# Two transformer layers with a sliding window: four attention blocks of the second layer taken in pairs

## The chip, the cores and the metric

The kernel runs on one core of one Trainium2 chip. The metric is the device time of one execution in microseconds, the median of several runs. The core's engines run side by side, each with an instruction queue of its own: TensorE (PE, with PEld for loading its stationary operand), VectorE (DVE), ScalarE (ACT), GpSimd (POOL) and SyncE (SP), which here only issues DMA transfers. An instruction that needs another engine's result waits for a semaphore, and everything behind it in its queue waits with it.

## The reference

Two attention layers and two MLPs alternate, with the same weights in both layers. S is 2048, D is 512, there are 32 heads of 16, and F is 1792.

```python
def _A_ref(x, wqkv, wo):
    B, S, D = x.shape
    H = 32; Dh = D // H; W = 256
    qkv = (lambda x, *d: x.transpose(*d))((x @ wqkv).reshape(B, S, 3, H, Dh), 2, 0, 3, 1, 4)
    q, k, v = qkv[0], qkv[1], qkv[2]
    scores = jnp.einsum("bhqd,bhkd->bhqk", q, k) * (Dh ** -0.5)
    idx = jnp.arange(S)
    mask = (idx[:, None] - idx[None, :] >= 0) & (idx[:, None] - idx[None, :] < W)
    scores = jnp.where(mask[None, None], scores, -1e9)
    p = _softmax(scores, axis=-1)
    o = jnp.einsum("bhqk,bhkd->bhqd", p, v)
    return (lambda x, *d: x.transpose(*d))(o, 0, 2, 1, 3).reshape(B, S, D) @ wo
...
x = x + _A_ref(_layernorm(x, axis=-1), A_wqkv, A_wo)
x = x + _B_ref(_layernorm(x, axis=-1), B_w1, B_b1, B_w2, B_b2)
```

The last two lines run twice. `_B_ref` is `gelu(h @ w1 + b1) @ w2 + b2` with the tanh form of gelu. A query sees itself and the 255 keys before it.

## The kernel before

**Tiles and blocks.** The 2048 tokens are 16 tiles of 128. Both layers together have 32 tiles (numbered 0 to 31) and 16 blocks of 256 queries (0 to 15); blocks 8 to 15 are the second layer. The 32 heads lie in four groups of eight (c = 0 to 3); a group's 128 channels fill the partitions.

**One block of attention (L730).** Keys are cut into tiles of 64. Key tile m of a block, counted from the block's first query, runs from -4 to 3 and meets the queries that `cols_of` (L707) gives it: 64 to 256 of them. The eight key tiles of a head group have 1280 columns together. They are packed into *visits* of exactly 512 columns (`pieces_of`, L711): ten visits per block, which hold 2, 2, 3, 3 and 6 (head group, key tile) units, twice over. In a visit PE does four matmuls of 32 rows per unit (L754), for the four pairs of heads of the group; two banks of PSUM at a time are then turned by ACT into exponentials in the ring E (L761, two instructions per visit), and masks of zeros and ones are multiplied onto the 64-column segments that lie on an edge of the window, by DVE or POOL (L782). When the five visits of two head groups are there, one product with V (L804, 128 small matmuls of 64 rows and 17 columns, the 17th a column of ones that gives the softmax sum) is made for both groups; then DVE transposes it out of PSUM (L813), takes reciprocals (L817), DVE or POOL normalises (L821), and DVE transposes again into OT (L827).

**Around it.** The output projection (`outproj`, L844) takes four matmuls per tile of 128 queries, and DVE adds the result to X (L849). Then follow the statistics on DVE (L599, L601), the reciprocal root on POOL (L611, L617), the normalised copy (L627) and a DMA transpose into xnTB (L632), which the MLP reads. The MLP runs in *jobs* of two or four tiles (`mlp`, L853; `JOBS`, L460); of the second layer's, tiles 16 to 19, 20 to 23 and 24 to 27 are jobs of four, 28 and 29 and 30 and 31 jobs of two. A job multiplies with w1 (L863), takes the gelu on ACT (L874, L879), multiplies with w2 (L892) and adds on DVE (L894); the second layer's tiles are then stored (L898). Tile 31 is done in two halves of 256 columns (L889). Q, K and V of a block are made two blocks ahead (L661, L680). All dense matmuls go through one helper and show as L653.

**Order.** Every instruction, or group of them, is a numbered node. `_ORDER` (L167) is one list of all node numbers, written out; each engine's queue is that list with the other engines' nodes left out. `_ALT` (L331) names the nodes that go to their second engine (masks and normalisations from DVE to POOL, some copies from PSUM to ACT, one step of the layer norm from POOL to DVE). `_BANKS` (L343) gives the PSUM bank of each group. The semaphores that a node waits for follow from what it reads and writes; a node waits for all of them before its first instruction. The product with V is one such node, and so is a visit.

Of the kernel before, what the change touches and what calls it, by code (L numbers as in the profile page):

```python
# [19 lines left out]
class _Sched:  # L20
# [147 lines left out]
    15, 34, 5, 0, 6, 14, 35, 7, 33, 28, 38, 29, 47, 8, 18, 23, 9, 36, 3, 26, 31, 10, 57, 37, 11, 22, 1, 40, 4, 24,  # L168
    2, 58, 59, 61, 17, 42, 62, 21, 60, 65, 41, 63, 19, 64, 68, 55, 32, 66, 107, 39, 69, 67, 20, 105, 50, 70, 3097,
    48, 30, 27, 53, 25, 106, 108, 71, 109, 49, 72, 110, 73, 16, 74, 114, 81, 75, 82, 111, 83, 84, 115, 85, 86, 116,  # L170
    112, 87, 88, 89, 113, 195, 153, 117, 127, 128, 151, 196, 129, 130, 154, 118, 152, 131, 119, 197, 155, 120, 156,
    98, 99, 100, 121, 12, 101, 90, 13, 102, 367, 91, 368, 104, 159, 92, 93, 157, 94, 103, 325, 76, 369, 199, 77,
    326, 95, 78, 200, 79, 370, 132, 80, 133, 96, 134, 135, 201, 323, 97, 203, 198, 137, 136, 158, 138, 205, 144,
    139, 202, 140, 145, 204, 141, 146, 160, 147, 122, 520, 217, 148, 123, 206, 124, 219, 143, 125, 208, 126, 46,
    218, 324, 43, 213, 209, 327, 328, 215, 166, 167, 168, 331, 169, 214, 207, 371, 176, 329, 177, 521, 373, 210,
    178, 330, 216, 179, 522, 171, 172, 180, 372, 161, 173, 211, 142, 174, 170, 56, 375, 220, 162, 376, 332, 163,
    164, 523, 175, 524, 221, 374, 377, 150, 212, 165, 149, 380, 378, 222, 188, 382, 189, 44, 190, 181, 45, 525,
    182, 381, 223, 385, 183, 224, 191, 386, 184, 384, 226, 225, 227, 54, 231, 232, 387, 379, 233, 526, 234, 383,
    333, 228, 185, 343, 388, 389, 334, 192, 229, 235, 344, 395, 194, 230, 335, 396, 345, 238, 346, 291, 390, 236,
    397, 239, 237, 347, 240, 336, 241, 348, 337, 349, 338, 242, 350, 244, 339, 243, 391, 399, 351, 401, 340, 341,  # L180
    352, 400, 245, 403, 342, 392, 402, 51, 353, 405, 52, 354, 355, 398, 356, 186, 360, 404, 357, 361, 362, 527,
    363, 393, 408, 364, 253, 409, 260, 261, 407, 254, 262, 410, 359, 413, 255, 246, 247, 415, 411, 256, 412, 257,
    248, 249, 250, 258, 414, 406, 564, 251, 273, 394, 274, 566, 263, 276, 416, 267, 268, 417, 565, 264, 270, 271,
    265, 277, 642, 285, 286, 423, 567, 418, 640, 275, 643, 528, 287, 529, 428, 272, 419, 282, 252, 283, 429, 288,
    259, 289, 641, 420, 308, 290, 309, 421, 424, 266, 310, 311, 279, 278, 644, 269, 422, 645, 284, 307, 280, 312,
    281, 313, 314, 315, 540, 425, 426, 568, 427, 541, 570, 316, 648, 542, 543, 649, 317, 569, 544, 318, 530, 531,
    319, 532, 187, 533, 572, 534, 193, 320, 574, 321, 646, 430, 431, 322, 647, 292, 573, 293, 294, 432, 577, 295,
    435, 579, 366, 576, 296, 545, 297, 436, 358, 571, 298, 433, 578, 546, 582, 434, 547, 437, 584, 548, 575, 550,
    438, 899, 551, 552, 650, 583, 553, 439, 651, 441, 652, 440, 653, 554, 900, 897, 585, 592, 654, 299, 549, 300,
    301, 593, 365, 302, 303, 304, 442, 581, 305, 594, 586, 535, 536, 898, 580, 596, 537, 306, 598, 538, 587, 901,  # L190
    539, 902, 597, 595, 600, 588, 557, 601, 660, 661, 662, 663, 599, 602, 605, 664, 558, 559, 607, 560, 655, 656,
    561, 457, 458, 606, 603, 610, 903, 657, 589, 658, 612, 904, 604, 453, 590, 459, 454, 476, 455, 477, 611, 485,
    486, 563, 609, 479, 591, 480, 482, 562, 613, 659, 470, 471, 483, 556, 905, 464, 465, 467, 478, 468, 484, 608,
    450, 460, 469, 461, 906, 451, 466, 446, 452, 447, 481, 443, 487, 448, 444, 473, 472, 462, 665, 474, 456, 614,
    666, 667, 445, 463, 615, 449, 475, 616, 684, 625, 626, 668, 617, 489, 686, 620, 618, 490, 491, 492, 685, 493,
    619, 621, 494, 669, 688, 687, 627, 690, 628, 622, 629, 495, 488, 623, 689, 496, 632, 692, 497, 694, 498, 624,
    691, 499, 500, 501, 630, 502, 693, 697, 504, 631, 505, 633, 1017, 506, 698, 507, 508, 634, 509, 1018, 510, 503,
    635, 699, 511, 702, 1019, 670, 512, 704, 700, 671, 672, 1020, 695, 673, 1021, 703, 674, 712, 696, 513, 514,
    701, 676, 714, 515, 706, 516, 517, 705, 518, 713, 519, 716, 638, 707, 717, 715, 718, 833, 720, 708, 721, 677,
    917, 1022, 918, 919, 709, 722, 920, 719, 710, 725, 921, 678, 727, 679, 680, 724, 681, 726, 730, 922, 636, 923,  # L200
    1023, 731, 912, 924, 728, 1024, 913, 723, 914, 915, 732, 729, 925, 711, 941, 637, 943, 734, 907, 908, 909, 733,
    910, 916, 926, 555, 735, 942, 639, 1025, 911, 736, 945, 934, 946, 935, 675, 737, 947, 738, 683, 949, 1026, 936,
# [763 lines left out]
```

## Time and profile before

| | |
|---|---|
| median of 3 runs | 442.32 us (442.26 to 442.40) |
| profiled execution, its own span | 442.4 us (442.375 us from the first to the last instruction) |
| granted clock of TensorE, mean | 0.996 of full speed |
| ACT_TABLE_LOAD instructions on ACT | 19, of 1.28 us each, nearly all at a change between exponential and gelu |
| score visits / products with V | 150 / 32 |
| mask instructions | 125 on DVE, 111 on POOL |

"Busy" is the time in which an engine has an instruction in work. Matmuls overlap: one of 512 columns is shown with about 0.38 us although the next begins 0.22 us after it, so what a group of matmuls costs is read from its start to the start of the next group, not from the durations. In a row of the timeline, x24 after an instruction is the number of them that are merged into the row; a few matmul records are missing from the trace, so a product with 128 matmuls may show fewer.

### The profile page before, as it was taken

How to read it: one execution, taken by the hardware profiler on the slowest of the kernel's cores; microseconds unless marked ns; L12 is line 12 of the kernel's file. 1: busy time of each engine (PE TensorE's matmuls, PEld its weight loads, DVE VectorE, ACT ScalarE, POOL GpSimd, SP SyncE). 2: the span in 40 equal slices, each digit the busy share in tenths (PEclk: the TensorE clock that was granted, in tenths of full speed). 3: DMA queues.
4: the chain of work that ended last, by engine and by line, in shares of the span. 5: the costliest groups of instructions: out<-in, count | busy, mean ns of one | idle time of the engine just before them, and what ended most of it. 6: DMA issues, size and time to landing. Idle time of an engine off the chain costs nothing.

```text
span 442.4 us, 16864 instructions
## 1 busy us (share of the span) xinstructions
PE 416.1 (94%) x7523; PEld 233.2 (53%) x7593; DVE 341.0 (77%) x638; ACT 386.4 (87%) x458; POOL 212.7 (48%) x236
## 2 busy tenths in 40 slices
PE   8997999988789997999999999999999999999997
PEld 4555657544444563554455455455555464444675
DVE  7997789788785599967698868877888576746762
ACT  4997999999889999889899989999897988999533
POOL 3566344363442674711575454634728165804411
PEclk9999999999899999999999999999999999999999
DMA  7686422004101012121031021100421014003002
GB/s 234 184 209 185 87 64 45 20 10 69 39 3 25 16 34 56 28 46 24 4 65 31 1 57 26 34 20 10 69 39 20 20 39 105 14 1 81 15 0 73
DMA packets 48116, 23.25 MB, mean 53 GB/s; under 512 B 33196, under 2 KB 48044, under 8 KB 48044
## 3 DMA queue, kind: packets, MB, share of 16 engines
q1 hardware_dynamic: 48044, 22.17, 22.2%
q8 instruction: 60, 0.98, 0.9%
q14 instruction: 12, 0.10, 0.1%
HBM read 8.00 MB, written 2.10 MB: 23 GB/s over the span
## 4 chain that ended last, share of the span: by engine, by line
PE 79%; ACT 11%; DVE 6%; issue 2%; DMA 1%; DVEq 0%
PE ps L653 59%; PE ps L754 9%; PE ps L804 9%; ACT E L761 9%; DVE OD L813 1%; PE ps L539 1%; DVE stat L599 1%; DVE X L849 1%; DMA xnTB<-xn 1%; ACT gT L879 1%; ACT L879 1%; DVE KT L687 1%; DVE E L782 0%; PE ps L639 0%; ACT QT L590 0%
## 5 line engine op out<-in xcount | busy, mean ns | idle before, releaser
L761 ACT ACTIVATE E<-ps 128x1024 bf16<-128x1024 f32 x300 | 284.2, 1033 | 28.7 <-PE ps L754 28.0
L782 POOL TENSOR_TENSOR E<-E,mask 128x512 bf16<-128x512 bf16 (+2 forms) x111 | 120.9, 1106 | 91.3 <-ACT E L761 91.0
L653 PE MATMUL ps<-W_sb,gT 128*128 128x512 bf16 (+1 forms) x434 | 112.2, 373 | 3.2 <-issue 2.2
L653 PE MATMUL ps<-xnTB,W_sb 128*128 128x512 bf16 (+1 forms) x541 | 107.8, 336 | 3.4 <-issue 1.8
L653 PEld LDWEIGHTS ps<-xnTB,W_sb 128*128 128x128 bf16 x560 | 52.0, 98 | 42.9 <-issue 4.1
L653 PE MATMUL ps<-xnTA,Wqkv_sb 128*128 128x256 bf16 x512 | 70.7, 273 | 0.9 <-ACT E L761 0.4
L782 DVE TENSOR_TENSOR E<-E,mask 128x512 bf16<-128x512 bf16 (+2 forms) x125 | 60.1, 500 | 13.3 <-ACT E L761 12.9
L754 PE MATMUL ps<-QT,KT 32*128 32x128 bf16 (+3 forms) x1920 | 60.3, 231 | 9.8 <-ACT E L761 5.6
L653 PEld LDWEIGHTS ps<-W_sb,gT 128*128 128x128 bf16 x462 | 41.2, 98 | 41.1 <-issue 3.6
L754 PEld LDWEIGHTS ps<-QT,KT 32*128 32x128 bf16 x1920 | 28.5, 92 | 59.1 <-ACT E L761 34.9
L653 PEld LDWEIGHTS ps<-xnTA,Wqkv_sb 128*128 128x128 bf16 x512 | 47.4, 98 | 20.2 <-issue 2.9
L813 DVE STREAM_TRANSPOSE OD<-ps 128x1024 f32<-128x1024 f32 x32 | 39.9, 1246 | 21.3 <-PE ps L804 20.7
L887 POOL TENSOR_TENSOR Xb<-X,b2all 128x512 f32<-128x512 bf16 x32 | 37.7, 1180 | 34.3 <-DVE X L894 33.9
L879 ACT ACTIVATE gT<-ps,b1T 128x512 bf16<-128x512 f32 (+1 forms) x80 | 42.6, 609 | 9.5 <-PE ps L653 9.4
L804 PE MATMUL ps<-E,Va 64*17 64x128 bf16 (+3 forms) x1920 | 44.3, 234 | 1.9 <-issue 0.8
L821 POOL TENSOR_TENSOR Nb<-OD,Rc 128x512 bf16<-128x512 f32 x25 | 26.4, 1058 | 38.7 <-DVE Rc L817 29.8
L804 PE MATMUL ps<-E,Vs 64*17 64x128 bf16 (+3 forms) x1920 | 44.9, 234 | 0.0
L599 DVE BATCH_NORM_STATS2 stat<-X 128x6 f32<-128x512 bf16 x64 | 42.9, 679 | 0.5
L804 PEld LDWEIGHTS ps<-E,Va 64*17 64x17 bf16 x1920 | 37.2, 85 | 11.6 <-issue 9.0
L871 DVE TENSOR_SCALAR gT<-ps,b1T 128x512 bf16<-128x512 f32 (+1 forms) x60 | 36.8, 632 | 6.6 <-PE ps L653 6.2
L687 DVE TENSOR_TENSOR KT<-ps,parmask 128x1024 bf16<-128x1024 f32 x32 | 38.7, 1211 | 3.6 <-PE ps L653 3.6
L804 PEld LDWEIGHTS ps<-E,Vs 64*17 64x17 bf16 x1920 | 38.0, 85 | 0.2
(55 smaller groups left out, 348.8 us busy)
## 6 DMA issues: line engine op xcount, KB each, us to landing
Vs<-Va SPq DMA_DIRECT2D x64, 68.0 KB, 2.0
W_sb<-in_B_w_dram SPq DMA_DIRECT2D x4, 512.0 KB, 4.8
out_dram<-X SPq DMA_DIRECT2D x15, 128.0 KB, 1.8
X<-in_A_x_dram SPq DMA_DIRECT2D x3, 512.0 KB
Wqkv_sb<-in_A_wqkv_dram SPq DMA_DIRECT2D x4, 256.0 KB, 4.5
W_sb<-in_B_w_dram SPq DMA_DIRECT2D x2, 384.0 KB, 7.1
W_sb<-in_B_w_dram SPq DMA_DIRECT2D x1, 768.0 KB, 5.0
Wqkv_sb<-in_A_wqkv_dram SPq DMA_DIRECT2D x1, 512.0 KB, 6.7
```

Source lines behind the costliest of these rows:

```text
L599: add("dve", lambda e, B, t=t, k6=k6: e.bn_stats(stat6[:, k6, :], X[:, t, :]), reads=["X%d" % t], writes=["st%d" % k6], key="bs%d" % (k + j))
L653: r = e.matmul(ps[:, B[g][0], cols], lhsT, rhs, start=st, stop=sp)
L687: add("dve", lambda e, B, g=g, i=i: e.tensor_tensor(out=KT[:, kb, 2 * i : 2 * i + 2].rearrange("p c m a q -> p a (c m) q"), in0=ps[:, B[g] ...
L754: x = e.matmul(ps[:, bk[r], o : o + n], KT[rows, kb, c, m].rearrange("p a q -> p (a q)"), QT[rows, c, q : q + n], start=True, stop=True)
L761: add("act", lambda e, B, g_=g_, gi=gi: e.activation(E[:, 2 * gi : 2 * gi + 2, e0 : e0 + 512], ps[:, B[g_][0] : B[g_][0] + 2, :], AF.Exp, ...
L782: fn = lambda e, B: e.tensor_tensor(out=Ew, in0=Ew, in1=Mw, op=ALU.mult)
L804: x = e.matmul(ps[32 * r : 32 * r + VW, B[g][par], c % 2 * 2 * P + lo : c % 2 * 2 * P + hi], V[rows, (2 * b + m // 2) % VR, c * HC + 2 * r ...
L813: add("dve", lambda e, B: e.transpose(OD[:, s].rearrange("p a c q -> p (a c q)"), ps[:, B[g][0] : B[g][0] + 2, :]), reads=["ps:" + g], wri ...
L821: return e.tensor_tensor(out=Nb[:, s, :].rearrange("p (k a d) -> p a k d", a=2, d=Dh), in0=sums[:, :, :, 0:Dh], in1=rc[:, :, :, None].to_b ...
L871: add("dve", lambda e, B, g=g, fc=fc: e.tensor_scalar(out=gT[:, fc, c0 : c0 + M], in0=ps[:, B[g][0], 0:M], scalar1=b1T[:, fc : fc + 1], sc ...
L879: add("act", lambda e, B, g=g, fc=fc: e.activation(gT[:, fc, c0 : c0 + M], ps[:, B[g][0], 0:M], AF.Gelu_apprx_tanh, bias=b1T[:, fc : fc + ...
L887: add("pool", lambda e, B, t=t, xs=xs: e.tensor_tensor(out=Xb[:, xs, :], in0=X[:, t, :], in1=b2all[:], op=ALU.add), reads=["X%d" % t, "b2a ...
```

## The change

Blocks 10 and 11 are taken as one block of 512 queries, and so are 12 and 13. In such a pair a key tile m runs from -4 to 7 and meets 64 to 320 queries; a head group has 2560 columns, in five visits of 512 that hold 2, 2, 2, 3 and 3 units. A product with V then serves one head group and 512 queries, with 96 matmuls, and fills the same two banks; there are four per pair, as there were four per two blocks. OT's two buffers hold the pair together, and the output projections of all four tiles follow the pair's products. K, Q and V of the next two blocks are both made ahead of a pair. A pair has 28 masks instead of 32: the visits with 3 units have one mask of four segments, and one mask of a single segment is of the kind that the other edge of the window needs.

```diff
+    PAIRS = (10, 12)
...
-        def cols_of(m):
-
-            return max(0, m) * HK, min(4, m + 5) * HK
+        def cols_of(m, nq):
+
+            return max(0, m) * HK, min(nq, m + 5) * HK
...
+            if b in PAIRS:
+                o = []
+                for c in range(DC):
+                    o += [[(c, -1), (c, 4)], [(c, -2), (c, 0)], [(c, 1), (c, 5)], [(c, -3), (c, 2), (c, 7)],
+                          [(c, -4), (c, 3), (c, 6)]]
+                return o
...
+                if pair:
+                    spans = ([(3, 1, 2)], [(2, 1, 2), (7, 1, -1)], [(0, 1, 1), (4, 1, 2)], [(1, 5, 4)], [(0, 5, 4)])[g % 5]
+                elif full:
...
+                elif k == 4:
+                    w0 = 0 if lo + 2 * step * HK <= NE else 3 * HK
+                    Ew = E[:, :, lo - w0 : lo - w0 + 2 * step * HK].rearrange(
+                        "p r (a k) -> p r a k", a=2)[:, :, :, w0 : w0 + 2 * HK]
+                    Mw = mask01[:, None, 0:2, :].rearrange("p r k n -> p r (k n)")[:, :, None, :].to_broadcast([P, RG, 2, 2 * HK])
...
-                for m in (0, 3, -1, -4, 1, 2, -3, -2):
-                    for c in (2 * cp, 2 * cp + 1):
+                for m in (0, 7, 1, 2, -4, 3, 4, 6, -3, -1, 5, -2) if pair else (0, 3, -1, -4, 1, 2, -3, -2):
+                    for c in (cp,) if pair else (2 * cp, 2 * cp + 1):
...
-            ends = {0: 5 if full else 3, 1: len(visits)}
+            ends = [5, 10, 15, 20] if pair else [5 if full else 3, len(visits)]
...
-            for j in range(2):
-                outproj(2 * b + j)
-            layernorm(b, 1, [(xnTB, t % 8 * P, "xb%d" % (t % 8)) for t in (2 * b, 2 * b + 1)])
+            for u in (b, b + 1) if pair else (b,):
+                for j in range(2):
+                    outproj(2 * u + j, pair)
+                layernorm(u, 1, [(xnTB, t % 8 * P, "xb%d" % (t % 8)) for t in (2 * u, 2 * u + 1)])
...
         for b in range(NB):
+            if b - 1 in PAIRS:
+                continue
...
+            for u in (b + 2, b + 3) if b in PAIRS else (b + 2,):
+                if u < NB:
+                    lnq(u)
+                    kv(u)
```

`_ORDER`, `_ALT` and `_BANKS` are new lists (3090 nodes instead of 3098). Read engine by engine, with the nodes counted off in program order, they say:

- Each engine's queue is the same as before up to the w2 products of tiles 8 and 9, in the last job but one of the first layer; from there on all five differ.
- The queues have 640 instead of 638 nodes on DVE, 222 instead of 232 on POOL, and the same numbers on PE (1629), ACT (439) and SP (160). Masks are 118 on DVE and 110 on POOL. Seven steps of the layer norm and two normalisations more are on DVE, and as many fewer on POOL.
- ACT has the same 300 exponentials and 110 gelus, in equally many stretches of the one and the other.
- In PE's queue dense work is followed by a visit or a product with V 83 times instead of 82.
- The masks of four segments are 12 on DVE and 4 on POOL.
- The projections of all four tiles stand behind all visits of their pair. Before, tile 21's stood in the middle of block 11's visits and tile 20's near their end, and those of 24 and 25 in the second half of block 13's.
- PE's queue ended with the w2 products of tile 30; it now ends with those of the second half of tile 31.

49 lines of the change are left out of this document (30 added, 19 removed), and 347 rows, old and new, of tables (_ALT, _BANKS, _ORDER).

## The prediction

> **What bounds the kernel now.** I read the page first: span, engines, chain by engine.
>
> ```profile
> span 442.4 us, 16864 instructions
> PE 416.1 (94%) x7523; PEld 233.2 (53%) x7593; DVE 341.0 (77%) x638; ACT 386.4 (87%) x458; POOL 212.7 (48%) x236
> PE 79%; ACT 11%; DVE 6%; issue 2%; DMA 1%; DVEq 0%
> ```
>
> PE leads, ACT is close behind. The share says little here, because the change has one place: read number by number against the order lists, all five queues are the same up to about 202 us (the w2 products of the first layer's tiles 8 and 9). So the second view is the busy time in stretches from there on, and the third the waits of PE in the same stretch.
>
> ```profile
> 202.00:250.00 48.00, 46.49 (x921) 23.77 (x928) 38.64 (x73) 44.51 (x51) 26.93 (x27) 1.00 0.14 29
> 250.00:300.00 50.00, 49.15 (x802) 25.77 (x809) 40.01 (x70) 47.30 (x55) 22.17 (x24) 1.00 0.14 31
> 300.00:350.00 50.00, 48.73 (x930) 25.75 (x938) 40.03 (x70) 44.37 (x51) 25.62 (x27) 1.00 0.22 35
> 350.00:400.00 50.00, 48.63 (x806) 24.48 (x814) 33.42 (x57) 45.91 (x52) 26.21 (x27) 1.00 0.16 40
> 400.00:442.40 42.40, 38.98 (x568) 25.31 (x557) 23.76 (x51) 22.19 (x35) 12.65 (x14) 1.00 0.13 39
> ...
> PE ps L653 <- issue: 4.0, 25, 0.2
> PE ps L754 <- ACT E L761: 0.2, 1, 0.2
> PE ps L653 <- DVE Va L588: 0.2, 1, 0.2
> ```
>
> Columns: PE, PEld, DVE, ACT, POOL busy, then the granted clock (1.00). In 240 us PE waits 0.4 us for other engines; the other 4.0 us are steps of at most 0.2 us after which nothing is late. PE's own work is the time in this half. **So the change gains only by what it takes out of PE's queue or off the end, and every new wait of PE costs in full.** There are no stalls left to remove: that caps the gain.
>
> **The change, part by part.** *Scores.* Per pair the twenty visits have 512 columns each as before, but hold 2, 2, 2, 3, 3 tiles of keys instead of 2, 2, 3, 3, 6. The six-tile visit (24 matmuls) goes, eight of them in the four blocks.
>
> ```profile
> 300.67 0.41 PE L754 MATMUL ps<-QT,KT 32*128 32x128 bf16 x24
> 301.01 1.68 PE L653 MATMUL ps<-W_sb,gT 128*128 128x512 bf16 x7
> 302.63 0.40 PE L754 MATMUL ps<-QT,KT 32*128 32x256 bf16 x8
> 302.96 0.60 PE L653 MATMUL ps<-W_sb,gT 128*128 128x512 bf16 x2
> ```
>
> Start to next start, 24 matmuls take 0.34 us and 8 take 0.33 us: columns are paid, instructions hardly. Saved: 8 x 0.01 = 0.08 us (0 to 0.08). The seven dense matmuls between take 1.62 us, some 0.22 us each and 0.1 us for going over to the tiled form. In PE's queue dense work is followed by a visit or an attention product 83 times instead of 82: +0.1 us (0 to 0.1).
>
> *Attention times V (L804).* One product per group of heads replaces one per two groups; their number stays four per two blocks, with 96 matmuls instead of 128, in twelve sets of eight that run side by side instead of sixteen.
>
> ```profile
> 317.10 0.28 PE L804 MATMUL ps<-E,Va 64*17 64x256 bf16 x4
> ...
> 317.33 0.20 PE L804 MATMUL ps<-E,Va 64*17 64x64 bf16 x4
> ...
> 317.40 0.30 PE L804 MATMUL ps<-E,Vs 64*17 64x256 bf16 x4
> ...
> 317.74 0.27 PE L804 MATMUL ps<-E,Va 64*17 64x192 bf16 x4
> ...
> 317.93 0.22 PE L804 MATMUL ps<-E,Vs 64*17 64x128 bf16 x2
> ...
> 318.18 0.27 PE L804 MATMUL ps<-E,Vs 64*17 64x192 bf16 x4
> ...
> 318.47 0.40 PE L754 MATMUL ps<-QT,KT 32*128 32x256 bf16 x8
> ```
>
> Two sets of 256 columns take 0.23 us, two of 64 take 0.07, two of 192 take 0.19, four of 128 take 0.25: 0.115, 0.035, 0.095 and 0.063 us a set. Before, four of each make 1.23 us of the 1.37 us to the next kind of work. After, there are two of each (0.615 us) and four of 320 columns, a width that the trace doesn't show. From 192 to 256 a set grows by 0.02 us, which gives 0.135; by columns from 256 it is 0.144. I take 0.135, the step from the nearest row: 1.155 us, 0.075 saved in each of eight products, **0.60 us**. The low end is 0.04 x 8 = 0.3 us. The high end is a price by instructions, 32/128 of 1.37 us, 0.34 x 8 = 2.7 us. A loss I leave out: a set costs less per column the wider it is.
>
> The Trainium skill, "TensorEngine Tiling (Array Packing)", Performance Considerations, gives each matmul an overhead of about 60 cycles. With 512 columns in 0.22 us that is an estimate of 0.026 us, so by it 16 matmuls fewer, four side by side, would make a visit 0.10 us shorter; the rows above show 0.01. The sum of scores and products by it would be 1.7 us instead of 0.68, and the time about 440.5.
>
> *Masks.* Eight fewer instructions (64 to 56) with the same elements; two visits in five now take one mask of four segments (1024 elements), a form not in the trace.
>
> ```profile
> L782 POOL TENSOR_TENSOR E<-E,mask 128x512 bf16<-128x512 bf16 x57 | 66.3, 1172 | 52.7 <-ACT E L761 52.7
> L782 POOL TENSOR_TENSOR E<-E,mask 128x768 bf16<-128x768 bf16 x17 | 29.9, 1764 | 11.2 <-ACT E L761 11.0
> L782 DVE TENSOR_TENSOR E<-E,mask 128x512 bf16<-128x512 bf16 x59 | 29.6, 513 | 4.7 <-ACT E L761 4.6
> L782 DVE TENSOR_TENSOR E<-E,mask 128x768 bf16<-128x768 bf16 x47 | 26.0, 571 | 8.3 <-ACT E L761 8.2
> ```
>
> On DVE (12 of the 16) it lies between 0.63 us (the step from 513 to 571 ns added) and 1.03 us (twice 513); on POOL (4) near 2.35 us by both ways. I take 0.63 and 2.35, the steps from the widest rows. Cost on the path: nothing, since DVE has 10 of 50 us idle and POOL 24. If that cover is gone, a late mask holds up its product. The shortest lead is at the last product of the second pair: its last visit starts 2 visits, 11 dense matmuls and two changes of form earlier, 0.66 + 2.4 + 0.2 = 3.3 us. It needs the 0.4 us of the visit, two exponentials and the mask.
>
> ```profile
> L761 ACT ACTIVATE E<-ps 128x1024 bf16<-128x1024 f32 x300 | 284.2, 1033 | 28.7 <-PE ps L754 28.0
> ```
>
> 0.4 + 2.07 + 0.63 (or 1.03) = 3.1 or 3.5 us: a wait of 0 to 0.3, taken as **0.15 us**. ACT has the same 300 exponentials, the same gelus and equally many changes between them, so it gains and loses nothing.
>
> *The end.* The queue now ends with the second half of the last tile instead of the whole tile before it.
>
> ```profile
> 439.39 0.69 DVE L894 TENSOR_TENSOR X<-Xb,ps 128x512 bf16<-128x512 f32 x1 [2.20 <-PE ps L653]
> ...
> L894 DVE TENSOR_TENSOR X<-Xb,ps 128x256 bf16<-128x256 f32 x2 | 0.8, 418 | 4.2 <-PE ps L653 4.2
> ...
> out_dram<-X SPq DMA_DIRECT2D x15, 128.0 KB, 1.8
> ...
> out_dram<-X SPq DMA_DIRECT2D x2, 64.0 KB, 1.7
> ```
>
> The addition behind the last matmul takes 0.42 instead of 0.69 us and the store 1.7 instead of 1.8: **-0.37 us** (-0.27 if the store gives nothing).
>
> *Moved.* The output projections of the first block of a pair (L847, tiles 20, 21, 24, 25) wait for the pair's last product; their residuals, statistics and DMA transposes then stand closer together on DVE, POOL and SP, ahead of the MLP job of that pair. Each job needs all four tiles in both kernels, so the move costs nothing while the transposes land in time; what it costs otherwise is the second rival.
>
> **Sum:** -0.60 - 0.08 + 0.10 + 0.15 - 0.37 = -0.80 us against the profiled 442.4, which stands 0.1 us over the median of 442.32: **441.5 us**. With all the small ends the sum is -0.2 us, with all the large ones -3.2. For this kernel 0.2% is 0.9 us, about what its measurement can tell from no change: the forecast lies at that edge.
>
> **The rivals.** *Paid by instruction* (439.4 us): a product takes 1.37 x 96/128. For it: the sets of 64 columns cost more per column than those of 256. Against: a set of 192 columns takes nearly three times one of 64, and the visits of 24 and 8 matmuls differ by 0.01 us. With 2.7 for 0.60 the sum is -2.9.
>
> *PE waits for the transposes ahead of the two pair jobs* (444 us, the other side). Place: the first w1 matmuls (L863) of the jobs of tiles 20 to 23 and 24 to 27.
>
> ```profile
> 319.02 1.03 PE L653 MATMUL ps<-Wo_sb,OT 128*128 128x512 bf16 x4 [0.16 <-issue]
> ...
> 330.24 1.03 PE L653 MATMUL ps<-xnTB,W_sb 128*128 128x512 bf16 x4 [0.16 <-issue]
> ...
> 324.87 3.07 SPq L632 DMA_TRANSPOSE xnTB<-xn  x2
> DMA to landing us min/median/max: 2.4/2.5/4.1
> ```
>
> Before, the last of these projections starts at 319.02 + 3 x 0.22 = 319.7 us; the second transpose is issued half-way through 3.07 us, at 326.4, and lands 2.5 us later, at 328.9. The chain takes 9.2 us, and PE comes to the job after 10.5. In the changed queue 23 dense matmuls, 4 visits, one product and 4 changes of form lie between: 5.1 + 1.3 + 1.3 + 0.4 = 8.1 us. With an unchanged chain PE waits 1.1 us, with the slowest landing 2.7. At the second pair the count is 25, 5, 1 and 5, 5.5 + 1.7 + 1.3 + 0.5 = 9.0 us, and two more transposes of 1.5 us each stand on SP, which makes the chain 12.2 unless two of them are issued while the projections still run; I allow 1.4 us there. Together 2.5 us, hence 444.0. It decides from where the chain at a job is longer than 8.1 or 9.0 us. Against it: the DVE queue of the changed kernel has no mask or cast between those residuals and the first pair's transposes, so its chain can be over a microsecond shorter.
>
> *It does nothing* (442.3 us): a 320-column set costs 0.144 us and small waits of 0.1 to 0.2 us at four or five short leads take back what the end gains.
>
> **How the numbers follow.** The forecast 0.57, the transposes 0.25, nothing 0.11, paid by instruction 0.07. The likeliest case has its own range of 441.0 to 442.0, half of it on either side of -0.2%. Faster by over 0.2%: 0.30 of the forecast and 0.07, 0.37. Slower by over 0.2%: the transposes, 0.25. Within: 0.38. The range reaches down past the estimate by columns to 440.5, which leaves out the price by instruction, and up to 444.3, past the transposes' middle, which leaves out about 0.1.
>
> **What would show it.** Right: a product of 96 matmuls takes 1.28 to 1.31 us to the next start; visits 0.33; PE's waits after 202 us on other engines stay under 0.8 us in all; the last addition takes 0.42 us. Wrong: a product near 1.03 us (by instruction); idle PE before L653 matmuls that read xnTB near 330 or 377 us, released by a DMA (transposes); L804 released by DVE or POOL masks of 1024 elements well over 0.63 and 2.35 us; or a difference that already stands at 202 us, where the queues are still the same.

## The result and the profile after

| | before | after |
|---|---|---|
| median of the runs | 442.36 us (442.26 to 442.56, 4 runs) | 446.47 us (445.52 to 447.46, 4 runs) |
| ratio, 95% interval | | 1.0096 (1.0078 to 1.0113) |
| profiled execution, span | 442.4 us | 445.2 us |

The change made the kernel about 1% slower, 4.1 us; the forecast was 441.5. The profiled execution of the changed kernel took 446.68 us: 1.5 us lie around its span (1.5 to 1.9 in the other executions of which both numbers are known). The two traces differ by 2.8 us only, because the profiled execution of before is not a typical one: for 3.4 us its clock was granted at half speed, and so it was in the profiled one of after, in the same place (116 to 120 us). Of the executions of the kernel before that were measured beside the experiments, 59 at the full clock took 442.2 us in the median and 10 with such a lowered clock 443.5. Of the four of after two had it lowered (446.68 and 447.46), two had not (445.52 and 446.26): compared like with like, the change costs about 3.6 us, and some 0.5 of the 4.1 belong to the clock. What follows compares like with like: the two traces.

Line numbers in rows of a kernel are its own: the dense matmul is L653 before, L647 after and L646 in most of the experiments, the product L804, L821 and L820. Three lines of the page of after (span, engines, chain by engine):

```profile
span 445.2 us, 16153 instructions
PE 425.5 (96%) x7209; PEld 231.1 (52%) x7209; DVE 343.0 (77%) x640; ACT 387.2 (87%) x458; POOL 212.7 (48%) x226
PE 76%; ACT 14%; DVE 5%; DMA 2%; issue 1%; POOL 1%; DVEq 0%; SPq 0%
```

Its busy time by stretch (columns: PE, PEld, DVE, ACT, POOL, clock), and PE's waits behind 202 us:

```profile
202.00:250.00 48.00, 45.77 (x917) 22.60 (x915) 36.96 (x64) 42.58 (x49) 27.06 (x25) 1.00 0.14 26
250.00:300.00 50.00, 49.70 (x652) 24.66 (x653) 38.32 (x70) 48.01 (x57) 22.66 (x21) 1.00 0.17 33
300.00:350.00 50.00, 49.04 (x753) 24.56 (x749) 39.02 (x74) 44.18 (x51) 21.95 (x21) 1.00 0.18 32
350.00:400.00 50.00, 49.81 (x751) 24.00 (x750) 35.34 (x59) 45.12 (x50) 28.30 (x27) 1.00 0.18 40
400.00:445.20 45.20, 42.40 (x590) 26.69 (x588) 27.65 (x55) 24.65 (x38) 11.27 (x12) 1.00 0.16 40
```

```profile
PE ps L647 <- issue: 1.1, 1, 1.1
PE ps L647 <- DVE QT L582: 0.6, 1, 0.6
PE ps L756 <- ACT E L763: 0.5, 1, 0.5
PE ps L821 <- DVE X L872: 0.4, 1, 0.4
PE ps L647 <- ACT E L763: 0.2, 1, 0.2
```

PE does less: 384 weight loads fewer (7209 instead of 7593). That it is "busy" for 9.4 us more comes from the records: in the trace of before 70 matmuls are missing (7523 rows to 7593 weight loads), in that of after none, and 4.7 of the 9.4 us lie ahead of 200 us, where both do the same work. The 25 steps of "issue" before, 4.0 us, come from there too: each stands where the record of the first dense matmul behind a visit or a product is missing. So a busy PE is no measure here; the waits say more. Before, other engines held PE up for 0.4 us in all behind 202 us; now it is 1.7 us in four waits, and a fifth, of 1.1 us, for which the view names no releaser, stands at 237 us, **ahead of the first pair**, where no pair is yet at work.

Small waits escape that view, so I also took PE's *loss*: from the start of each node of PE's queue to the start of the next, less its normal pitch (a dense matmul 0.216 us, a visit 0.333, a product 1.37 or, in a pair, 1.22, and 0.1 for going over from dense to tiled), added up by stretch. This is worked out from the starts in the traces, in us:

```
kernel                 200-220 220-240 240-260 260-300 300-320 320-340 340-400 400-440   sum
before                     0.4     0.3     0.0     0.2     0.0     0.2     0.5     0.0   1.6
after                      0.5     2.9     0.0     0.8     0.5     0.9     0.6     0.3   6.5
e1_tx45_first              0.5     1.8     0.0     1.0     0.5     0.8     1.6     0.3   6.4
e2_before_tx45_late        0.5     1.8    -0.2     0.3    -0.1     0.2     0.3     0.2   3.0
e3_pairs_behind_old..      0.6     0.8     1.5     0.8     0.3     1.2     0.7     0.1   5.9
e4_before_with_new..       0.4     2.7     2.3     0.0     0.3     0.1     0.5     0.2   6.4
e6_pairs_reordered         0.6     0.4     0.1     2.4     1.2     1.3     2.2     0.8   8.9
e9_old_order_then_mended   0.5     0.3     0.5     0.9     0.2     2.3     0.9     0.4   6.1
e12_after_4_fewer..        0.5     1.5     0.1     1.2     0.3     0.8     0.4     0.3   5.2
e13_both_causes..          0.5     1.0    -0.2     1.3     0.5     0.6     1.3     0.4   5.4
```

The traces then add up. After loses 4.9 us more; its eight products save 8 x 0.15 = 1.2 us and its visits 0.1; the additional change of form costs 0.1; at 204 us it was 0.6 us ahead; and from the last matmul to the end it needs 0.4 us less. 4.9 - 1.2 - 0.1 + 0.1 - 0.6 - 0.4 = 2.7, and the traces differ by 2.8.

**The larger half, 220 to 240 us.** SP's queue, before and after (start, duration; one row may hold several DMAs):

```profile
204.48 2.50 SPq L632 DMA_TRANSPOSE xnTB<-xn  x2
...
225.02 2.53 SPq L632 DMA_TRANSPOSE xnTA<-xn  x2
...
230.61 2.50 SPq L632 DMA_TRANSPOSE xnTB<-xn  x2
```

```profile
203.84 1.19 SPq L626 DMA_TRANSPOSE xnTB<-xn  x1
223.58 2.50 SPq L626 DMA_TRANSPOSE xnTA<-xn  x2
...
228.01 1.27 SPq L626 DMA_TRANSPOSE xnTB<-xn  x1
...
231.41 2.50 SPq L626 DMA_TRANSPOSE xnTB<-xn  x2
```

These are the transposes of tiles 12 to 15 into xnTB, which the last job of the first layer reads. Before, tiles 12 and 13 went off together at 204.5 us. After, tile 13's stands behind the two transposes of block 11 into xnTA. Those wait at 203.8 to 223.6 us for their buffer, and tile 13's waits with them, though its data lay ready by 203.8 us. It lands at 230.5; only then is its buffer of xn free, the next two copies on DVE start at 230.60, tiles 14 and 15 go off at 231.4 and 232.6, and the job waits:

```profile
235.21 0.82 PE L647 MATMUL ps<-Wo_sb,OT 128*128 128x512 bf16 x3
237.16 0.38 PE L647 MATMUL ps<-xnTB,W_sb 128*128 128x512 bf16 x1 [1.13 <-issue]
```

The transpose of tile 15, issued at 232.64, should have landed 2.5 us later, at 235.1. Each transfer reports 16 landings: fifteen came after at most 2.53 us, the sixteenth after 4.43. Between them a 16 KB packet of the program's own code started at 235.06 and ran 0.93 us:

```profile
q8 instruction: 57, 0.93, 0.9%
```

57 packets in 445 us are 0.9% of the DMA time and look like nothing. But of the 391 transposes behind 200 us in the fourteen traces of this case, 103 took over 3 us, and a code packet overlapped every one of the 103; of the other 288 one overlapped 58. What matters is when the packet starts: all 82 transposes whose packet started 0.55 to 2.2 us behind their issue took over 3 us, but only 4 of the 29 whose packet started 2.2 to 2.5 us behind it. Tile 15's, with 2.42, is one of the four.

Not all of the 2.9 us are these transposes. Tile 13's late landing held up DVE's copies and so a product of block 9 (idle 0.43 us at 233.4; with the transpose moved back, in e1, that wait is gone), tile 15's the job (1.13); a visit at 228.0 waited 0.46 us for an exponential on ACT, and the rest is in smaller steps.

**The smaller half, in and behind the pairs.** The product of a pair in the timeline, from its first row to the next visit, and the two masks of four segments in the view by forms:

```profile
318.68 0.31 PE L821 MATMUL ps<-E,Va 64*17 64x320 bf16 x4
...
319.90 0.40 PE L756 MATMUL ps<-QT,KT 32*128 32x320 bf16 x8
```

```profile
L798 DVE TENSOR_TENSOR E<-E,mask 128x1024 bf16<-128x1024 bf16 x12 | 8.9, 758 | 1.0 <-ACT E L763 1.0
L798 POOL TENSOR_TENSOR E<-E,mask 128x1024 bf16<-128x1024 bf16 x4 | 8.5, 2136 | 10.0 <-ACT E L763 10.0
```

1.22 us for 96 matmuls against 1.37 for 128. Where the gain goes is to be seen on DVE around the end of the second pair's first product:

```profile
321.30 0.69 DVE L872 TENSOR_TENSOR X<-X,ps 128x512 bf16<-128x512 bf16 x1
322.02 0.69 DVE L593 BATCH_NORM_STATS2 stat<-X 128x6 f32<-128x512 bf16 x1
322.63 0.77 DVE L621 TENSOR_SCALAR xn<-X,statmv,rstd 128x512 bf16<-128x512 bf16 x1
323.32 0.67 DVE L917 TENSOR_TENSOR X<-Xb,ps 128x512 bf16<-128x512 f32 x1
323.92 0.64 DVE L621 TENSOR_SCALAR xn<-X,statmv,rstd 128x512 bf16<-128x512 bf16 x1
324.49 0.68 DVE L582 CAST QT<-ps 128x512 bf16<-128x512 f32 x1
```

DVE works without a gap: a residual and the statistics of a tile of the first pair, two normalised copies for block 14, an addition of the MLP, and last the cast of Q, which frees the bank that PE needs; PE waits 0.6 us for it at 325.2. And the transposes of tiles 24 to 27, ahead of their job, go off in one piece (SP, after; then before, where they are spread over 20 us):

```profile
374.65 5.41 SPq L626 DMA_TRANSPOSE xnTB<-xn  x4
```

```profile
354.53 1.19 SPq L632 DMA_TRANSPOSE xnTB<-xn  x1
...
364.32 1.21 SPq L632 DMA_TRANSPOSE xnTB<-xn  x1
...
371.89 2.51 SPq L632 DMA_TRANSPOSE xnTB<-xn  x2
```

The fourth was issued at 378.80 and landed 2.48 us later, at 381.3; the job began at 381.5, and PE lost 0.3 us there.

### The profile page after: what moved, and what is told of

Same layout as the page of the kernel before. It is cut to its first block, busy times and chain, and to the rows that moved or that the text cites. A ratio compares the mean times of both kernels' runs of the same rounds, so it can differ in the third digit from the quotient of the medians.

```text
span 445.2 us, 16153 instructions
## 1 busy us (share of the span) xinstructions
PE 425.5 (96%) x7209; PEld 231.1 (52%) x7209; DVE 343.0 (77%) x640; ACT 387.2 (87%) x458; POOL 212.7 (48%) x226
## 4 chain that ended last, share of the span: by engine, by line
PE 76%; ACT 14%; DVE 5%; DMA 2%; issue 1%; POOL 1%; DVEq 0%; SPq 0%
PE ps L647 58%; ACT E L763 12%; PE ps L821 9%; PE ps L756 8%; DMA xnTB<-xn 2%; DVE OD L830 1%; ACT gT L902 1%; PE ps L533 1%; DVE E L798 1%; DVE X L872 1%; POOL E L798 1%; ACT gT L897 1%; DVE xn L621 1%; DVE stat L593 1%; DVE gT L894 0%
## 5 line engine op out<-in xcount | busy, mean ns | idle before, releaser
L798 POOL TENSOR_TENSOR E<-E,mask 128x512 bf16<-128x512 bf16 (+3 forms) x110 | 124.0, 1143 | 98.4 <-ACT E L763 98.3
L647 PE MATMUL ps<-W_sb,gT 128*128 128x512 bf16 (+1 forms) x462 | 116.0, 374 | 0.8 <-DVE QT L582 0.6
L647 PE MATMUL ps<-xnTB,W_sb 128*128 128x512 bf16 (+1 forms) x560 | 112.4, 338 | 2.6 <-issue 1.1
L647 PEld LDWEIGHTS ps<-xnTB,W_sb 128*128 128x128 bf16 x560 | 52.2, 98 | 43.7 <-issue 6.1
L647 PE MATMUL ps<-xnTA,Wqkv_sb 128*128 128x256 bf16 x512 | 72.6, 273 | 0.3 <-ACT E L763 0.2
L756 PE MATMUL ps<-QT,KT 32*128 32x128 bf16 (+4 forms) x1792 | 60.4, 236 | 8.8 <-ACT E L763 5.3
L647 PEld LDWEIGHTS ps<-W_sb,gT 128*128 128x128 bf16 x462 | 41.1, 98 | 42.9 <-issue 4.4
L798 DVE TENSOR_TENSOR E<-E,mask 128x512 bf16<-128x512 bf16 (+3 forms) x118 | 55.9, 494 | 8.2 <-ACT E L763 8.0
L647 PEld LDWEIGHTS ps<-xnTA,Wqkv_sb 128*128 128x128 bf16 x512 | 46.9, 98 | 21.9 <-issue 3.2
L838 POOL TENSOR_TENSOR Nb<-OD,Rc 128x512 bf16<-128x512 f32 x23 | 24.4, 1062 | 58.8 <-DVE Rc L834 38.1
L821 PE MATMUL ps<-E,Va 64*17 64x128 bf16 (+4 forms) x1792 | 43.0, 239 | 2.3 <-issue 0.8
L821 PE MATMUL ps<-E,Vs 64*17 64x128 bf16 (+4 forms) x1792 | 43.4, 238 | 0.0
L821 PEld LDWEIGHTS ps<-E,Va 64*17 64x17 bf16 x1792 | 35.5, 85 | 12.7 <-issue 10.2
L917 DVE TENSOR_TENSOR X<-Xb,ps 128x512 bf16<-128x512 f32 (+1 forms) x33 | 22.0, 669 | 21.7 <-PE ps L647 21.4
```

Source lines behind the costliest of these rows:

```text
L647: r = e.matmul(ps[:, B[g][0], cols], lhsT, rhs, start=st, stop=sp)
L756: x = e.matmul(ps[:, bk[r], o : o + n], KT[rows, kb, c, m].rearrange("p a q -> p (a q)"), QT[rows, c, q : q + n], start=True, stop=True)
L798: fn = lambda e, B: e.tensor_tensor(out=Ew, in0=Ew, in1=Mw, op=ALU.mult)
L821: x = e.matmul(ps[32 * r : 32 * r + VW, B[g][par], co + lo : co + hi], V[rows, (2 * b + m // 2) % VR, c * HC + 2 * r + par, :], E[rows, r, ...
L838: return e.tensor_tensor(out=Nb[:, s, :].rearrange("p (k a d) -> p a k d", a=2, d=Dh), in0=sums[:, :, :, 0:Dh], in1=rc[:, :, :, None].to_b ...
```

## The experiments

The expectations count the kernels by the number in the name; no kernel has the number 5. Where an order is moved, the diff names nodes by their keys. In the keys, and in some of the expectations, transposes into xnTB count from 32: tx45 and tx47, "tile 45" and "tile 47" there, are tiles 13 and 15, and the job they feed is that of tiles 12 to 15 (the last expectation but one calls it that of tiles 16 to 19). All ratios are to the kernel before on the same chip.

**e1_tx45_first**: the changed kernel, one transpose moved on SP.

```diff
   tx44
+  tx45
   tx23
   tx22
   vs20_1
   vs19_1
-  tx45
   vs19_0
```

> The changed kernel with one node of the order list moved: the DMA transpose of tile 13 (tx45) is issued on SP right behind that of tile 12, ahead of the transposes of tiles 6 and 7 of the second layer and two copies of V. In the profile of the changed kernel tx45 stood behind transposes that wait for a buffer until 223.6 us, was issued at 228.0 us and landed at 230.5; DVE, the product of block 9 and the job of tiles 12 to 15 waited, some 2.9 us of PE between 226 and 238 us. Theory A (the order of SP's queue ahead of the pairs makes most of the loss): 443.5 to 444.5 us, and runs that lie closer together. Theory B (the pairs themselves cost it): 446 to 447 us, as without the move, since the wait only moves elsewhere.

445.70 us (444.39 to 446.70), ratio 1.0072 (1.0054 to 1.0091): 0.8 us back, where theory A expected 2 to 3; the interval overlaps the changed kernel's, so the times alone do not settle it. The wait of block 9's product went; but tile 15's transpose, now issued at 232.2, still met a code packet (at 234.12) and landed after 4.0 us, and 0.87 us of the wait at the job stayed. Of what was won, the trace shows 0.9 us given back at the job of tiles 24 to 27: a code packet met the first of the four transposes, and SP needed 2.35 us for the second instead of 1.2.

**e2_before_tx45_late**: the reverse in the kernel before.

```diff
   tx44
-  tx45
   vs19_0
   tx23
   tx22
   vs19_1
+  tx45
```

> The kernel before, without pairs, with the same one node moved the other way: tx45 behind the transposes of tiles 6 and 7 of the second layer and a copy of V on SP. Theory A: 2 to 3 us slower than before, 444.5 to 445.5 us, with PE idle ahead of the job of tiles 12 to 15. Theory B: within 0.5 us of the kernel before, 442.4 us.

443.40 us (442.48 to 444.79), ratio 1.0023 (1.0012 to 1.0034). One DMA late on SP costs a kernel without any pair 1.1 us, less than the 2 to 3 of theory A, and the loss appears where it does after: 1.6 us between a visit and the job of tiles 12 to 15.

```profile
229.97 2.53 SPq L625 DMA_TRANSPOSE xnTB<-xn  x2
...
233.49 0.41 PE L747 MATMUL ps<-QT,KT 32*128 32x192 bf16 x12
235.56 1.24 PE L646 MATMUL ps<-xnTB,W_sb 128*128 128x512 bf16 x5 [1.66 <-DVE OD L806]
```

The row names DVE, whose OD was done at 235.04; by the times it is tile 15's transpose. Issued at 231.28, it met a code packet (at 233.18) and landed after 3.98 us, at 235.26. After the usual 2.5 us it would have landed at 233.8, just as the visit ended. Before, it landed 1.1 us ahead of the end of that visit. So here the moved DMA used up the slack, and the packet made the wait.

**e3_pairs_behind_old_order**: the changed kernel's code; up to the first visit of block 10 (1661 nodes) the order of before, from there that of after.

> The pairs with all queues as in the kernel before up to the first visit of block 10 (about 237 us), and what is left in the order of the changed kernel. Theory A: the loss ahead of the pairs is gone (3.5 us with the small waits at 216 to 233 us); what stays is the gain of the products (8 x 0.15 us by the profile of the changed kernel), of the end (0.3 us) and the waits of some 1.5 us between 280 and 335 us: 442 to 443 us. Theory B: 446 us, and PE waits near the pairs as large as the loss.

444.86 us (444.47 to 445.53), ratio 1.0058 (1.0044 to 1.0072): 1.6 us back, between the two theories. The loss of 220 to 240 us went (0.8); 1.5 us came in where the two orders were joined (240 to 260), which is this kernel's own. The losses in and behind the pairs stayed as they were.

**e4_before_with_new_order_ahead**: the counterpart; the kernel before with after's order up to the first visit of block 10 (1695 nodes), then its own.

> The kernel before, computing exactly what it did, with the changed kernel's order of work from the start up to the first visit of the first pair's place (block 10) and its own order from there on. Theory A, the reordering ahead of the pairs is what the changed kernel pays: in its trace PE loses 2.9 us beyond its normal pitch between 220 and 240 us where the kernel before loses 0.3, and it was 0.3 to 0.6 us ahead at 202 us; so this kernel, which has no pairs at all, takes 444.5 us (443.8 to 445.2), and the transposes of tiles 45 to 47 are again issued behind those of tiles 23 and 22. Theory B, the pairs themselves cost the time: 442.3 us (441.9 to 442.8).

447.55 us (446.54 to 447.62), ratio 1.0110 (1.0094 to 1.0125). No pair, and as slow as the changed kernel (the intervals overlap). 2.7 us are lost between 220 and 240 as in after, with the same wait at the job, whose tile 15 landed after 4.34 us with a code packet at 234.06. Another 2.3 us are lost at this kernel's join. Its time alone would exaggerate theory A; the stretch 220 to 240 shows it.

**e7_after_8_fewer_warmups**: the changed kernel, all work in its order.

```diff
-        for h in range(NWARM):
+        for h in (0, 1, 3, 4, 5, 6, 7, 8, 13, 15):
```

> The changed kernel without eight of the eighteen warm-up products at the very start (seven of 32 columns, one of 512; their result is used nowhere): PE's instruction stream is eight products shorter ahead of everything, the work and its order stay. Theory F: each 16 KB packet of the instruction queue sits for about 1 us on one of the 16 DMA engines, and the share of a transpose that queues behind it lands up to 2 us late; in the changed kernel's trace such a packet started at 235.06 us, the transpose of tile 47 had 15 of its 16 landings after 2.53 us and the last after 4.43 us, and PE idled 1.13 us for it. With the packet later by eight products it comes behind that transpose: the last landing after about 2.5 us, the idle time ahead of the first product of that block below 0.3 us, time 445.3 us (444.7 to 445.9). Rival G: two transposes issued one behind the other hold each other up (or the wait is the fourth block's own): landing again above 4 us, idle time about 1.1 us, time 446.5 us.

450.24 us (449.81 to 451.27), ratio 1.0180 (1.0164 to 1.0196). The wait that it was made for went: the last landing of tile 15's transpose came after 2.54 us, and the job no longer waited (the product ahead of it waited 1.1 us instead of 0.4). But the packet had not moved behind the transpose: it started 2.41 us after its issue, in after 2.42. And the time went the other way, by 3.8 us. Up to 94 us this trace is level with that of after (first visit at 10.62 us against 10.69), so the 1.7 us in the first 20 us of which the expectation of e11 speaks are not to be seen in the starts. Then, in the middle of a product of the first layer, PE stood still:

```profile
95.40 0.28 PE L820 MATMUL ps<-E,Va 64*17 64x128 bf16 x5
97.78 0.26 PE L820 MATMUL ps<-E,Va 64*17 64x192 bf16 x3 [2.10 <-issue]
```

Nothing on the page releases it; a code packet had started at 95.36 us, and the one in its place in after at 91.58. By 102 us this execution was 3.1 us behind that of after, and 3.0 at its end: the whole difference arises here. That PE had run out of code is the likely reading; no view states it. A product puts 128 matmuls and as many weight loads into 1.4 us, more instructions in a time than anything else here.

**e6_pairs_reordered**: e3 with 278 nodes moved on their queues behind 200 us (PE 153, DVE 73, ACT 22, POOL 17, SP 13), chosen by replaying the queues with the durations of the traces.

> The changed kernel's code (pairs, masks of four segments and all) with a third order: the third run's (the kernel before up to the pairs, the changed kernel from there), in which nodes behind 200 us were moved a few places on their queues so that the waits of PE that the traces name go: the join of the two orders, the first query-key visits and products of each pair, the jobs behind the pairs. Theory A, the pairs in themselves save 0.15 us in each of eight products, 0.1 us in the visits and 0.3 us at the end, and all that the change paid was queue order: 440.8 us (440.2 to 441.5), PE's loss beyond its pitch under 2 us from 200 us on where the changed kernel has 6.5. Theory B, the pairs bring waits of their own that no order removes (four projections and eight transposes that wait for one product): 442.3 us or more.

447.58 us (447.42 to 447.83), ratio 1.0122 (1.0105 to 1.0139): worse by far than e3, and beyond what either theory spoke of. The join went (0.1), but from 260 us on it lost 7.9. Its rows on DVE, POOL and PE show what the replay did not know:

```profile
314.84 1.23 DVE L620 TENSOR_SCALAR xn<-X,statmv,rstd 128x512 bf16<-128x512 bf16 x1 [0.82 <-POOL rstd L610]
315.99 0.68 DVE L797 TENSOR_TENSOR E<-E,mask 128x1024 bf16<-128x1024 bf16 x1
...
314.77 1.15 POOL L909 TENSOR_TENSOR Xb<-X,b2all 128x512 f32<-128x512 bf16 x1
...
317.13 0.31 PE L820 MATMUL ps<-E,Va 64*17 64x320 bf16 x4 [1.16 <-DVE rstd L604]
```

The copy takes 0.40 us elsewhere in this trace (at 316.60, for one). Here it began while POOL added, and ended 0.15 us after POOL did; the mask behind it was late by that much, and so was the product. The trace names a statistics step as releaser; by the times it is the mask, which ended at 316.67: PE's queue passed the first of its waits at 316.76 and took until 317.08 for the three behind it. The Trainium skill, "SBUF — State Buffer", Who interferes with whom, says that DVE's two-port modes, which a TENSOR_SCALAR can enter, use a port pair shared with GpSimd, and that whoever comes first has it for the whole instruction while the other waits. The row agrees, and so do the others of its kind: of the 896 normalised copies in the fourteen traces 72 began inside a POOL instruction of over 0.6 us; 68 of them took over 0.5 us, and 67 of these ended 0.15 us after it. The other 824 took 0.41 us in the median.

**e8_before_reordered**: the control, 112 nodes of the kernel before moved by the same replay.

> The control: the kernel before with its nodes behind 200 us moved in the same way, no pairs. PE loses 1.6 us there beyond its pitch, so at most that is to be had: 441.6 us (440.9 to 442.4). Theory A: this stands 0.5 to 1.5 us above the reordered pairs. Theory B: it stands below them.

444.04 us (443.38 to 444.48), ratio 1.0041 (1.0026 to 1.0056). Reordered without that knowledge, the kernel before became slower too (2.4 us of loss behind 200 us instead of 1.6, and 0.8 more just ahead of it). By the letter this is theory B, since it stands 3.5 us below e6. But as the same replay harmed a kernel without pairs, e6's rise cannot be put down to the pairs.

**e9_old_order_then_mended**: e3 with 36 nodes moved, chosen by a replay in which the fast copies, masks and normalisations of DVE and POOL's work exclude each other. On DVE for example:

```diff
   vp52
-  xn52
   mk12_4_0
+  xn52
   xn53
```

> The third run's kernel (pairs; the order of before up to the first visit of block 10, the changed kernel's from there) with 36 nodes moved on their queues behind 200 us, most by a few places: 11 on DVE (among them the masks mk10_4 and mk12_4, the residual rs22, the gelu input gb6_0), 19 on PE, 3 on ACT, 2 on SP, 1 on POOL, chosen so that no mask or normalised copy on DVE meets more POOL work than before (where they met in the sixth kernel, a copy of 0.41 us took 1.23). Theory A, what the third run still lost (444.9 us, some 4 us of PE beyond its pitch from 240 us on) is queue order, not the pairs: 442.5 us (441.8 to 443.3), PE's loss from 240 us on under 2.5 us. Theory B, the pairs' own waits cannot be ordered away: 444.5 us or more, the wait of the first product of pair 12 and of the job of tiles 24 to 27 still there.

445.12 us (444.07 to 446.57), ratio 1.0065 (1.0040 to 1.0091); theory B's side, and no better than e3. The join fell from 1.5 to 0.5 us and the wait of the second pair's first product went. In return the place at 320 us doubled, to 2.3: the transposes of tiles 20 and 21 met a code packet at 316.83 (4.36 and 4.11 us), a normalised copy on DVE waited 0.7 us for their buffer and took 1.37, and the cast of Q stood behind it. At the job of tiles 24 to 27 the wait rose from 0.3 to 0.9.

**e10_after_mended**: the changed kernel with 41 nodes moved in the same way.

> The changed kernel with 41 nodes moved on their queues behind 200 us (16 on PE, 20 on DVE, 2 on ACT, 2 on POOL, 1 on SP), its order otherwise kept, the late transpose of tile 45 too. Theory A: 444.2 us (443.4 to 445.0), of the 2.9 us lost between 220 and 240 us about half stays, since SP's order stays. Theory B: 446 us or more.

446.21 us (444.75 to 447.99), ratio 1.0088 (1.0063 to 1.0112); theory B's side, and not to be told from the changed kernel. Its loss between 220 and 240 fell from 2.9 to 1.9, and 0.8 came in between 320 and 340, 0.6 at the job of tiles 24 to 27.

**e11_before_8_fewer_warmups**: e7's edit in the kernel before.

> Control of the seventh run's kernel: the kernel before without the same eight warm-up products at the start, nothing else. That run rose by 3.8 us although its wait at tile 47 went: its trace has 1.7 us more loss in the first 20 us and a 2.4 us stop of PE inside a product at 95 us, where a packet of its own code was just coming in. Theory H, the missing warm-ups do that whatever stands behind 200 us: this kernel takes 445.5 us (444.5 to 446.5). Rival, the seventh run's rise lies in the pairs: 442.3 us (441.9 to 442.8).

446.01 us (444.64 to 447.53), ratio 1.0075 (1.0054 to 1.0095): 3.4 us, theory H. Five of the six executions had a lowered clock; the sixth took 444.64, still 2.4 us more than before at the full clock. PE's waits up to 110 us, before and in this kernel (the product is L804 there and L796 here):

```profile
PE ps L804 <- issue: 0.8, 2, 0.6
```

```profile
PE ps L796 <- issue: 3.1, 3, 2.3
```

The same stop inside a product, with no change behind it, and again the packet there is late: it starts at 95.13 us, before at 91.47. Behind 200 us this kernel loses 1.8 us, as before.

**e12_after_4_fewer_warmups**: a smaller dose in the changed kernel.

```diff
-        for h in range(NWARM):
+        for h in (0, 1, 3, 4, 5, 6, 7, 8, 9, 11, 12, 13, 14, 15):
```

> The changed kernel without four of its warm-up products (32 columns each, results unused), so that its code comes in four products later, with the start nearly as it was. Theory F: the code packet that held up the transpose of tile 47 comes behind it, the last landing after 2.5 us instead of 4.4, the idle time of 1.13 us ahead of the job of tiles 16 to 19 under 0.3; 445.3 us (444.6 to 446.0) where nothing else is hit. Rival G, the transpose is late of itself: idle time and 446.4 us unchanged.

444.96 us (444.23 to 446.58), ratio 1.0055 (1.0037 to 1.0072); the time of theory F, 1.5 us below the changed kernel with the same work in the same order. All six executions had the full clock; against the two such of after it is 0.9. SP and PE, in this kernel:

```profile
230.39 2.50 SPq L625 DMA_TRANSPOSE xnTB<-xn  x2
...
234.42 0.59 PE L646 MATMUL ps<-Wo_sb,OT 128*128 128x512 bf16 x2 [0.16 <-issue]
234.85 0.38 PE L646 MATMUL ps<-xnTB,W_sb 128*128 128x512 bf16 x1
```

The transposes are issued 1.0 us earlier than in after, as everything is in this execution, mainly because its clock was not lowered at 116 us; tile 15's lands after 2.56 us, and the job begins 4.5 us behind their issue instead of 5.8, without the idle 1.13. So the transpose is not late of itself, and rival G is out. But the mechanism of theory F is not shown either: the packet started at 234.01, 2.38 us behind the issue, as close as in after, and this time held up no landing. At this distance few are held up (4 of 29, above); what decides it is open.

**e13_both_causes_ahead_removed**: e1 and e12 together.

> The changed kernel with both of the causes named ahead of the pairs taken out: the transpose of tile 45 right behind tile 44's (the first run, 0.8 us back) and four warm-up products fewer at the start (the run before this one, 1.4 us back). Theory: the two are different waits, so they add: 444.2 us (443.4 to 445.0), PE's loss between 220 and 240 us under 1.3 us where the changed kernel has 2.9, and what stays over the kernel before lies in the pairs' own waits behind 260 us. Rival: they are one wait seen twice: 445 us, no better than the better of the two.

445.24 us (443.53 to 445.81), ratio 1.0066 (1.0050 to 1.0083). The loss of 220 to 240 fell to 1.0 as expected, so the two waits are different ones. The time did not follow, it is the rival's 445: at the job of tiles 24 to 27 SP was held up as in e1 (2.08 us for the second transpose), the fourth landed at 379.0, as late as in e12 (378.9) although PE was there 0.5 us earlier, and 0.88 us were lost instead of 0.26.

## Why the prediction was wrong

**Where the bound was right.** "Every new wait of PE costs in full" held: the ledger above closes with PE's losses and nothing else. That no other engine held PE up behind 202 us was read rightly too; the 4.0 us of small steps were no waits at all, but gaps in the records.

**The step that failed: "Moved".** The prediction costed only the projections of tiles 20, 21, 24 and 25, and the queues ahead of the pairs at nothing, although the list of what changed says that all five queues differ from the first layer's last jobs on. Ahead of the pairs the new order put one transpose behind two that wait 20 us for a buffer. That transpose and the two behind it came late: a product waited 0.43 us and the job of tiles 12 to 15 another 1.13, because the last of them, with no slack left, met a packet of code. With a visit that waited 0.46 us for ACT and smaller steps the new order lost 2.6 us more here than the old, more than the 1.05 us of gains that the forecast had counted. That the order is the cause is shown by e4 (2.7 us in this place with no pair), e2 (one DMA moved in a kernel without pairs, +1.1 us) and e3 (0.8 instead of 2.9 with the old order ahead); that the late landing has its own part, by e12 and e13, whose traces have neither it nor the wait at the job.

**Products, 0.60 us.** The mechanism was right, the size too small: 0.15 us each instead of 0.075, 1.2 us in all, between the two ends of 0.3 and 2.7. The sets of 320 columns were not cheaper than the 0.135 us taken; the rest of a product took less than the sum of its sets.

**Scores, masks, the end.** Visits of 8 and 12 matmuls took 0.33 us, as forecast. A mask of four segments took 0.68 us on DVE in the undisturbed cases (758 ns is the mean) and 2.14 on POOL, forecast 0.63 and 2.35. The last addition took 0.42 us and the end 0.4 less, forecast 0.37.

**The rival of the transposes.** Its first place came to 0.3 us instead of 1.1. Its second was right in kind: four transposes in one piece on SP, 0.3 us lost; in e1, e9 and e13, where a code packet held up SP's issue of the second one too, 0.9 to 1.2, against the 1.4 allowed. It was not the main cause.

**The wait at the last product of the second pair, 0.15 us,** did not come; the first product waited instead (0.2 us, in e3 and after alike), as did the matmuls that need the bank of Q (0.65) and a visit and the matmul behind it at 282 us (0.4): the work of four tiles and two coming blocks meets on DVE. From 240 us on after loses 2.2 us more than before, against 1.3 saved in products and visits and 0.4 at the end: the pairs' own part comes out as a loss of about 0.5 us in these two traces.

**What stays open.** Whether an order exists in which the pairs gain: none of the six orders tried with them came below 444.8. e6, e9 and e10 removed waits and received others; that no order can is not shown. Nor is it shown what decides whether a packet that starts just ahead of a landing holds it up, or why the packet of 91 us came 3.7 to 3.8 us later in e7 and e11. There is one trace of each kernel, while executions of the changed kernel differ by 1.9 us.

**The anchor.** The profiled 442.4 was set beside the median of 442.32 as if it were the same kind of number. With the 1.7 to 1.9 us that lie around the spans of this kernel, a span of 442.4 belongs to a time of about 444.2; the typical execution of before has a span of about 440.6. For a forecast by differences this changed nothing, but the two traces could not show the whole 4.1 us.

## What to carry to other kernels

When an order is written out anew, compare every queue from the first difference on, SP's above all: ask of each DMA what stands ahead of it and what that waits for, before costing the instructions that the change is about. In kernels like these a DMA whose data are needed less than two microseconds after its usual landing has no slack: 103 of 391 transposes came 0.5 to 2.2 us late beside a packet of the program's own code. In an order this tight a wait removed by hand was often the cover of the next one (e1, e6, e9, e13), so count a gain only at the end.

## What the runs showed of the hardware

- Code is fetched in 16 KB packets, 57 to 60 in an execution, about 1.1 us each. The transposes that landed after 3.0 to 4.7 us instead of 2.4 to 2.5 were each overlapped by one; those whose packet started 0.55 to 2.2 us behind the issue were all late. The Trainium skill, "Runtime: NRT & Kernel Launch", Instruction fetch mechanics, says that engines refill their code in 16 KiB blocks of 256 instructions over a DMA queue and that this is mostly hidden. The size agrees, and so does the count, if the packets are PE's: 57 for 14418 matmuls and weight loads in after, 60 for 15186 in before, one for 253 in both. In these kernels it was not hidden (1.13 us at a job, 2.10 us inside a product).
- So a change of a few unused instructions at the start moves the time: four fewer took 1.5 us off the changed kernel (0.9 at equal clock), eight fewer put 3.8 on it and 3.4 on the kernel before. A difference of 1% between two such kernels need not come from what was changed.
- A normalised copy on DVE that begins inside a POOL instruction of over 0.6 us ends 0.15 us after it (67 of 72): one of 0.40 us took 1.23.
- In e6 a product began 0.46 us after the mask that it had waited for longest: PE's queue took from 316.76 to 317.08 us for the three waits behind that one.
